# Threshold attention with a feed-forward on one core: the first four head pairs computed with queries on partitions, the first feed-forward blocks ordered one 256-token block at a time, and new ranks

## The chip, the cores and the metric

The kernel runs on one core of one Trainium2 chip. The metric is the time of one execution in microseconds (us). Of the kernel before, three runs are known: 1312.47, 1314.48 and 1315.28 us, median 1314.48 us.

Five engines matter here. TensorE (PE in the profile, its weight loads PEld) multiplies matrices into PSUM, VectorE (DVE) and ScalarE (ACT) work on tiles in SBUF and PSUM, GpSimd (POOL) and SyncE (SP) issue most DMA transfers. The program holds a list of instructions for each engine, which waits on semaphores where it needs another engine's result.

## The reference

There are 8 batches, 8 heads, 576 tokens and head dimension 64; the attention output, 4608 tokens by 512, is the input of a feed-forward of width 2048.

```python
scores = scale * np.matmul(q, k.transpose(0, 1, 3, 2))
thresh = np.max(scores, axis=-1, keepdims=True) - tau
scores = np.where(scores >= thresh, scores, -1000000000.0)
scores = scores - np.max(scores, axis=-1, keepdims=True)
attn = np.exp(scores)
attn = attn / (np.sum(attn, axis=-1, keepdims=True) + 1e-09)
out = np.matmul(attn, v)            # then (B,H,S,D) -> x (B*S, H*D)
h = x @ w_in                        # 512 -> 2048
g = h * (1.0 / (1.0 + np.exp(-1.702 * h)))
return g @ w_out                    # 2048 -> 512
```

q, k and v are float32. The two weight matrices arrive as float64, and the kernel makes float32 of them itself.

## The kernel before

**Pairs.** Two heads form a pair; there are 32 pairs, n = 0 to 31, four to a batch. A pair goes through a row of steps. Its q and k are loaded (`load_qk`, SP) and turned on VectorE (`prep`, L522). The scores are computed with keys on partitions: for each of nine groups of 64 keys, four matmuls of a quarter of the array each (`scores`, L538) fill one of three PSUM buffers called `psA`. ScalarE copies each group to SBUF (`keep`, L555), as five tiles, four of 128x1152 and one of 128x576. The maximum over keys therefore runs across partitions: VectorE reduces while it turns 32x32 blocks (`in_groups`, L561), then over tiles and halves (`over_tiles`, `over_halves`), turns the small result, writes it to DRAM and reads it back spread over all partitions (`row_out`, `row_in`; pair 2 spreads it on VectorE). VectorE subtracts it from the tiles (`sub`, L666), ScalarE masks with a steep Prelu (`mask`, L672) and takes exponentials (`exps`, L676). TensorE multiplies by v (`values`, L687). For pairs 0 to 4 the sums are matmuls with ones (`sums_by_pe`, also L687) that VectorE reduces, inverts and spreads (`one_row`, `spread_sums`); later pairs sum on VectorE and spread through DRAM. `place_x` (L789) writes the normalised result, transposed, into the tiles `xT` of 256 tokens that the feed-forward reads.

**Weights.** 32 pieces of 128x512, 16 of `w_in` and then 16 of `w_out`, are each loaded by two 512 KB transfers from POOL (`load_w`) and converted in four steps: three on VectorE (`cv_ex` L484, `cv_frac` L498 and L502, `cv_end` L510) and one on ScalarE (`cv_power` L492). The first six loads are held back by a small POOL copy (`hold`, L529) that waits until k of pair 3 is turned.

**Feed-forward.** Blocks of 256 tokens. The first two blocks go together as plain matmuls (`first_blocks`): for each of 16 column groups j of `w_in`, four matmuls for block 0 and four for block 1 (`mm1_0`, L844), into a PSUM buffer of the pool `psM`, of which there are two; a tanh on ScalarE and a product on VectorE (`gelu_0`, L850); then the second layer (`mm2`, L826). All of it waits for the four pairs of batch 0. Blocks from 2 on (`feed_forward`, L804 and L995) use seven products in place of eight; block 2 needs pairs 0 to 7.

**Who sets the order.** Nothing is executed as it is written down. Each step is a task with an engine, a planned cost, a rank, prerequisites and buffer counts that it takes and gives (`task`). `run_in_order` plays the tasks through in planned time: an engine that is free takes the ready task of lowest rank whose buffers are free, and the instructions are emitted in that order. Ranks are the pair's number plus a bias by function name from a table: `EARLY` for pairs 0 to 3, `SECOND` for 4 to 7, `LATER`, and `CV` and `W_RANK` for the weights. Feed-forward matmuls have the highest rank and fill what TensorE has left over. From pair 7 on, the values of pair n-2 and the scores of pair n alternate tile by tile.

Of the kernel before, what the change touches and what calls it, by code (L numbers as in the profile page):

```python
# [30 lines left out]
def kernel(  # L31
# [75 lines left out]
        for x in range(2)  # L107
# [9 lines left out]
    minus = const.tile([P, 2, KT], FP32, name="minus")  # L117
    own_row = const.tile([P, QB // 2], FP32, name="own_row")
    shift = const.tile([P, 1], FP32, name="shift")

# [6 lines left out]
    limits = {"psA": 3, "psM": 2, "s_m": 8, "s_t": 2, "io": 2, "hs": 2, "osb": 2, "xT": NXT, "mb": 1,  # L127
              "raw0": 1, "raw1": 1, "qkT0": 1, "qkT1": 1, "v_m0": 1, "v_m1": 1, "w64_0": 1, "w64_1": 1, "row": 1, "row_s": 1, "rc": 1}
    for x in ("raw0", "raw1", "qkT0", "qkT1", "mb"):
        limits[x + "_apart"] = 1  # L130
    limits["s_m_apart"] = NKT

    EARLY = {
        "exps": -17.61,
        "in_groups": 12.77,
        "keep": 26.48,
        "load_qk": 6.42,
        "load_v": 0.46,  # L140
        "mask": 4.73,
        "one_group": -15.86,
        "one_row": -9.06,
        "over_halves": -11.42,
        "over_tiles": -0.06,
        "place_x": -9.61,
        "prep": -11.56,
        "row_in": 31.26,
        "row_out": -12.68,
        "scores_run": 26.41,  # L150
        "spread_max": 4.27,
        "spread_sums": 4.87,
        "sub": 8.56,
        "sums_by_pe": -5.69,
        "sums_in": 2.27,
        "sums_out": 16.51,
        "turn_rows": -16.86,
        "turn_sums": -5.4,
        "values": 24.67,
        "w_sum": 2.1,  # L160
        "x_sum": -20.63,
    }
    SECOND = {
        "exps": -12.92,
        "in_groups": 29.73,
        "keep": 6.19,
        "load_qk": 1.9,
        "load_v": 13.07,
        "mask": 1.29,
        "one_group": 2.55,  # L170
        "one_row": -2.79,
        "over_halves": -24.79,
        "over_tiles": 9.26,
        "place_x": -19.31,
        "prep": -22.42,
        "row_in": -9.56,
        "row_out": -26.33,
        "scores_run": 2.45,
        "spread_max": 6.39,
        "spread_sums": -1.67,  # L180
        "sub": 27.62,
        "sums_by_pe": 38.88,
        "sums_in": 16.9,
        "sums_out": 8.98,
        "turn_rows": 12.04,
        "turn_sums": -0.33,
        "values": 2.02,
        "w_sum": -3.88,
        "x_sum": -12.22,
    }  # L190
    LATER = {
        "exps": 1.49,
        "in_groups": 1.97,
        "keep": -9.78,
        "load_qk": -5.98,
        "load_v": -3.59,
        "mask": 21.95,
        "one_group": 4.78,
        "one_row": -20.84,
        "over_halves": 8.94,  # L200
        "over_tiles": -3.1,
        "place_x": 4.68,
        "prep": -7.1,
        "row_in": 2.23,
        "row_out": -2.52,
        "scores_run": -13.43,
        "spread_max": -3.68,
        "spread_sums": -27.9,
        "sub": 9.4,
        "sums_by_pe": 4.28,  # L210
        "sums_in": 8.55,
        "sums_out": -0.12,
        "turn_rows": -4.72,
        "turn_sums": 8.12,
        "values": 0.63,
        "w_sum": 21.55,
        "x_sum": 7.65,
    }
    CV = {
        "cv_end": -26.29,  # L220
        "cv_ex": 6.34,
        "cv_frac": -13.49,
        "cv_power": -9.91,
        "load_w": 3.03,
# [4 lines left out]
    QUARTERS = ("scores", "scores_run", "again", "values", "sums_by_pe")  # L229
    ENTER = {True: 0.2, False: 0.22}  # L230

    def task(engine, cost, rank, f, *a, after=(), take=(), give=(), lag=None):
        if lag is None:
            lag = LAG[engine]
        if 0 <= rank < LAST:
            biases = EARLY if a[0] < NPAIR else SECOND if a[0] < 2 * NPAIR else LATER
            rank += CV[f.__name__] if f.__name__ in CV else biases.get(f.__name__, 0.0)
        tasks.append((engine, cost, rank, f, a, [x for x in after if x is not None],
                      take, give, lag))
        return len(tasks) - 1  # L240
# [14 lines left out]
    def run_in_order():  # L255
# [30 lines left out]
        while events:  # L286
# [24 lines left out]
            for engine, queue in ready.items():  # L311
# [24 lines left out]
                if engine == "PE":  # L336
                    held_for = follows.get(i)
                    last, mode = mode, tasks[i][3].__name__ in QUARTERS
# [7 lines left out]
    TWICE = ()  # L346
    BY_POOL = {}

    APART = (1, 3)
    spare = arena[:, 8 * P * 4 :]
    offset = {"raw0": 0, "raw1": S, "qkT0": 2 * S, "qkT1": 3 * S, "mb": 4 * S}
    offset.update({f"s_m{t}": (6 + 2 * t) * S for t in range(NKT)})
# [17 lines left out]
    def home(n, tag, key=None):  # L372
        if n in APART:
            o = offset[key or tag]
            return spare[:, o : o + (2 if tag == "s_m" else 1) * S]
        return seat(tag)

    def seat_scores(n, t):

        if t < NKT and n in APART:  # L380
            return home(n, "s_m", f"s_m{t}")
# [13 lines left out]

    def own(n, *pools):
        return tuple(x + "_apart" for x in pools) if n in APART else pools

# [18 lines left out]
    def load_v(n):  # L417
        b, hp = divmod(n, NPAIR)
        t = seat("v_m", n % 2).rearrange("p (h j d) -> p h j d", j=NK, h=2)
# [99 lines left out]
    def prep(n, which):  # L519

        dst = home(n, f"qkT{which}")
        nc.vector.transpose(out=dst, in_=raws.pop((n, which)))  # L522
        mats[n, which] = dst
        if which:
            held_k[n] = dst
# [8 lines left out]
    def scores(n, j):  # L534
# [8 lines left out]
        if j == NK - 1 and n not in TWICE:  # L543
# [33 lines left out]
    def over_halves(n):  # L577
# [7 lines left out]
        if n in TWICE:  # L585
            for x, y in ((0, 0), (1, 2), (2, 1), (3, 3)):
                nc.vector.scalar_tensor_tensor(
                    out=flat[0][ts(y, 32), 0:QB], in0=r[ts(x, 32)], scalar=gap[ts(x, 32)],
                    in1=o[ts(x, 32)], op0=ALU.subtract, op1=ALU.max,
                )  # L590
            return
# [14 lines left out]

    def row_blocks(n):

        nc.vector.transpose(out=flat[1], in_=flat[0])
        mb = home(n, "mb")[:, 0:SH]  # L610
        nc.vector.tensor_tensor(
            out=mb.rearrange("p (g i) -> p g i", i=32),
            in0=flat[1].unsqueeze(1).to_broadcast([P, QB // 2, 32]),
            in1=own_row.unsqueeze(2).to_broadcast([P, QB // 2, 32]), op=ALU.mult,
        )
        mbs[n] = mb

    def again(n, j):
        ps = psA.tile([P, 2, 512], FP32, name="ps", tag="ps")
        for first in (True, False):  # L620
            for h in range(2):
                for c in range(2):
                    if first:
                        left = mats[n, 1][ts(h, D), ts(j, KT)]
                        right = mats[n, 0][ts(h, D), ts(c, SH)]
                    else:
                        left, right = minus[ts(h, D), c, :], mbs[n][ts(h, D), :]
                    nc.tensor.matmul(
# [863 lines left out]
```

## Time and profile before

| what | value |
|---|---|
| median of three runs | 1314.48 us (1312.47 to 1315.28) |
| span of the profiled execution | 1309.8 us |
| median above the span | 4.7 us |
| PE busy over the span | 1260.5 us, 96% |
| DVE, ACT, POOL busy | 1002.2, 646.6, 246.1 us |
| first feed-forward matmul (L844) | at 113.93 us |
| first matmul of block 2 (L804) | at 273.55 us |
| mean granted TensorE clock | 0.989 |

The profile gives the span of the profiled execution, from its first to its last instruction. A run's time also holds what lies around that span; no time of the profiled execution itself is given, so the 4.7 us are the distance from this span to the median of the runs. Busy time is the union of an engine's instructions. The trace holds two records for each f32 matmul, so a count there is twice that of the program. The last batch's end is the end of TensorE's work, so the two marks at 113.93 and 273.55 us cut the span into an attention stretch, a mixed stretch, and the long rest.

### The profile page before, as it was taken

Reading aid. Unit: us, or ns where it says so; the run is one execution under the profiler, and the core shown is the slowest. Engines: PE = TensorE matmul, PEld = TensorE weight load, DVE = VectorE, ACT = ScalarE, POOL = GpSimd, SP = SyncE. Lnnn points to the kernel's source line nnn. Section 1 sums busy time; section 2 is a strip of 40 time slices with the busy share of each in tenths; the row PEclk is TensorE's granted clock in tenths of the full one; section 3 lists DMA queues with packets and bytes.
Section 4 is the critical chain, followed back from the end, with each engine's and each line's share of the span. In section 5 each row is a group of like instructions: output and inputs, shape, how many; then the busy total and the mean of one; then the engine's idle time right before and its main releaser. Section 6 shows DMA issues by size and latency. Waiting matters only on the chain. (4 is left out here: it accounts for less than half of the span.)

```text
span 1309.8 us, 22824 instructions
## 1 busy us (share of the span) xinstructions
PE 1260.5 (96%) x9128; PEld 972.6 (74%) x9128; DVE 1002.2 (77%) x1601; ACT 646.6 (49%) x830; POOL 246.1 (19%) x300
## 2 busy tenths in 40 slices
PE   5869999999999999999999999999999999999998
PEld 2436854477688777777778888777777778888887
DVE  7999998989998877778877877777888864652642
ACT  5975656766664544455554545454556540210210
POOL 1301210022030212112020302020212117120120
PEclk8989999999999999999999999999999999999999
DMA  6976967264322222221222222222122110000000
GB/s 118 339 186 214 282 209 132 67 125 83 82 57 71 55 64 64 56 57 44 63 47 61 55 71 55 72 56 70 42 52 54 38 44 9 9 1 33 1 1 32
DMA packets 194309, 103.78 MB, mean 79 GB/s; under 512 B 160284, under 2 KB 171292, under 8 KB 194204
## 3 DMA queue, kind: packets, MB, share of 16 engines
q1 hardware_dynamic: 180476, 64.30, 20.6%
q0 software_dynamic: 11360, 37.74, 9.7%
q8 instruction: 71, 1.16, 0.4%
q10 hardware_dynamic: 2368, 0.30, 0.2%
q14 instruction: 34, 0.28, 0.1%
HBM read 88.40 MB, written 9.70 MB: 75 GB/s over the span
## 5 line engine op out<-in xcount | busy, mean ns | idle before, releaser
L561 DVE TRANSPOSE_TENSOR_REDUCE part<-arena 128x36 f32<-128x1152 f32 x295 | 361.5, 1241 | 45.9 <-ACT arena L555 32.3
L804 PE MATMUL hps<-xT,w_in 128*128 128x256 f32 x1536 | 336.9, 380 | 0.4 <-DVE arena L816 0.4
L804 PEld LDWEIGHTS hps<-xT,w_in 128*128 128x128 f32 x1536 | 290.8, 190 | 45.5 <-issue 5.7
L672 ACT ACTIVATE arena<-arena 128x1152 f32<-128x1152 f32 (+1 forms) x160 | 169.4, 1058 | 144.9 <-DVE arena L666 144.6
L555 ACT COPY arena<-ps 128x576 f32<-128x576 f32 x288 | 170.4, 647 | 121.2 <-PE ps L538 120.9
L666 DVE TENSOR_TENSOR arena<-arena 128x1152 f32<-128x1152 f32 (+1 forms) x158 | 197.5, 1281 | 19.6 <-DMA arena<-row 19.5
L995 PE MATMUL ops<-w_out,arena 128*128 128x256 f32 x896 | 202.9, 381 | 1.2 <-DVE arena L816 1.1
L676 ACT ACTIVATE arena<-arena,shift,scl 128x1152 f32<-128x1152 f32 (+1 forms) x160 | 200.1, 1251 | 4.1
L538 PE MATMUL ps<-arena 64*64 64x288 f32 x2304 | 174.1, 419 | 25.1 <-DVE arena L522 14.4
L995 PEld LDWEIGHTS ops<-w_out,arena 128*128 128x128 f32 x896 | 169.0, 190 | 29.1 <-DVE arena L816 3.7
L961 POOL TENSOR_TENSOR arena<-arena 128x256 f32<-128x256 f32 x56 | 50.8, 907 | 658.4 <-DVE arena L816 556.7
L687 PE MATMUL pv<-arena 64*64 64x288 f32 x2176 | 161.2, 410 | 0.0
L538 PEld LDWEIGHTS ps<-arena 64*64 64x64 f32 x2304 | 83.7, 137 | 93.6 <-ACT arena L555 30.7
L995 PE MATMUL ops<-arena 128*128 128x256 f32 x672 | 150.6, 380 | 0.0
L813 ACT ACTIVATE th<-hps 128x512 f32<-128x512 f32 x112 | 66.0, 589 | 167.9 <-PE hps L804 148.2
L995 PEld LDWEIGHTS ops<-arena 128*128 128x128 f32 x672 | 127.3, 190 | 19.3 <-issue 2.2
L687 PEld LDWEIGHTS pv<-arena 64*64 64x64 f32 x2176 | 82.0, 135 | 55.3 <-issue 12.8
L1017 DVE SCALAR_TENSOR_TENSOR osb<-ops,osb 128x256 f32<-128x256 f32 x98 | 39.5, 414 | 91.8 <-PE ops L995 85.0
L816 DVE SCALAR_TENSOR_TENSOR arena<-th,hps 128x512 f32<-128x512 f32 x96 | 64.1, 667 | 37.1 <-ACT th L813 37.0
L844 PE MATMUL hps<-xT,w_in 128*128 128x256 f32 x256 | 57.3, 382 | 1.3 <-DVE arena L850 1.2
L826 PE MATMUL ops<-w_out,arena 128*128 128x512 f32 x128 | 56.4, 596 | 0.0
L844 PEld LDWEIGHTS hps<-xT,w_in 128*128 128x128 f32 x256 | 48.1, 190 | 11.0 <-DVE arena L850 3.0
(117 smaller groups left out, 1027.8 us busy)
## 6 DMA issues: line engine op xcount, KB each, us to landing
arena<-in_v_dram SPq DMA_DIRECT2D x128, 144.0 KB
arena<-in_q_dram SPq DMA_DIRECT2D x128, 72.0 KB
out_dram<-osb SPq DMA_DIRECT2D x36, 256.0 KB
arena<-in_k_dram SPq DMA_DIRECT2D x124, 72.0 KB
arena<-row SPq DMA_DIRECT2D x62, 144.0 KB
arena<-row_s SPq DMA_DIRECT2D x54, 144.0 KB
w_out<-in_moe_w_in_dram POOLq DMA_DIRECT2D x12, 512.0 KB, 9.4
arena<-in_moe_w_out_dram POOLq DMA_DIRECT2D x12, 512.0 KB, 5.9
```

The lines of the kernel that those rows point to most:

```text
L538: nc.tensor.matmul(ps[ts(c, KT), h, 0:SH], lhsT=mats[n, 1][ts(h, D), ts(j, KT)], rhs=mats[n, 0][ts(h, D), ts(c, SH)], start=True, stop=True,)
L555: nc.scalar.copy(out=sT[n, t][:, u], in_=pss.pop((n, j))[:, :, 0:SH])
L561: nc.vector.tensor_reduce(out=stats[n, op][:, t * 2 * QB : min(2 * t + 2, NK) * QB], in_=sT[n, t].rearrange("p u h (g d) -> p (u h g) d", ...
L666: engine.tensor_tensor(out=s, in0=s, in1=mbs[n].unsqueeze(1).to_broadcast(list(s.shape)), op=ALU.subtract)
L672: nc.scalar.activation(out=s, in_=s, func=AF.Prelu, alpha=STEEP)
L676: nc.scalar.activation(out=s, in_=s, func=AF.Exp, scale=scl, bias=shift)
L687: nc.tensor.matmul(o[c][ts(h, D), 0:SH], lhsT=left(j, h)[ts(c, KT)], rhs=sT[n, t][ts(c, KT), u, h, :], start=(j == 0), stop=(j == NK - 1),)
L804: nc.tensor.matmul(hidden[j][:, ts(f, BLK)], lhsT=w_in[:, c, ds((f * HF + j) * P, P)], rhs=xTs[blk][:, c, :], start=(c == 0), stop=(c == N ...
L813: nc.scalar.activation(out=ths[j], in_=hidden[j], func=AF.Tanh, scale=GELU_SCALE / 2)
L816: nc.vector.scalar_tensor_tensor(out=g[:, :, j, :], in0=two(ths.pop(j)), scalar=1.0, in1=two(hidden.pop(j)), op0=ALU.add, op1=ALU.mult,)
L844: nc.tensor.matmul(hidden[j][:, ts(i, BLK)], lhsT=w_in[:, c, ts(j, P)], rhs=xTs[i][:, c, :], start=(c == 0), stop=(c == NDC - 1),)
L995: nc.tensor.matmul(banks[blk][k][:, ts(o, HM)], lhsT=left[:, j, :], rhs=right[:, j, :], start=(j == 0), stop=(j == HF - 1),)
```

## The change

1. **Pairs 0 to 3 are computed the other way round.** For each pair and each tile of 128 queries (four whole tiles and one of 64 queries, so 20 units in all) `straight_scores` puts queries on partitions and keys along the row. The row maximum is then one VectorE reduction from PSUM per head (`straight_max`), and its negative plus tau a bias per partition (`straight_bias`). ScalarE masks from PSUM with that bias (`straight_mask`) and takes exponentials with the row sum as a second output (`straight_exps`). Ten transposes by TensorE per whole unit turn the exponentials (`straight_turn`), into one `psA` and one `psM` buffer, ScalarE copies them out (`straight_copy`, `straight_copy1`), VectorE inverts the sums (`straight_rc`), TensorE spreads them (`straight_den`) and multiplies by v (`straight_values`), ScalarE copies the spread (`straight_spread`) and VectorE multiplies (`straight_place`). Gone for these pairs are `keep`, `in_groups`, the trip of the maxima through DRAM, `sub`, the 1152-wide `mask` and `exps`, `sums_by_pe`, `one_row`, `spread_sums` and `place_x`.
2. **Order of units.** Token tiles 0 and 1 of all four pairs come first (units 0 to 7), then tiles 2 to 4. All q and k of the four pairs are loaded first, into the arena; v is loaded twice per pair.
3. **First feed-forward blocks.** The order is now layer 1 of block 0, layer 1 of block 1, layer 2 of each. Block 0 waits only for tiles 0 and 1 of the four pairs.
4. **Ranks and planned costs.** All bias tables, `CV` and `W_RANK` have new numbers, some planned costs are changed, so the emitted order of every engine is new to the end. Pairs 4 to 31 and blocks from 2 on keep their instructions.

```diff
+    def straight_scores(n, t):
+        qT, kT = mats[n, 0], mats[n, 1]
+        ps = [psA.tile([P, 2, 512], FP32, name="ps", tag="ps") for _ in range(heads(t))]
...
+        for h, c, kk in runs:
+            o = t * P + (c * KT if heads(t) == 2 else 0)
+            nc.tensor.matmul(
+                ps[h % heads(t)][ts(c, KT), kk, 0:SH], lhsT=qT[ts(h, D), ds(o, KT)],
+                rhs=kT[ts(h, D), ts(kk, SH)], start=True, stop=True,
+            )
...
+    def straight_max(n, t, h):
+        nc.vector.tensor_reduce(
+            out=figures(n, t, 0)[:, h : h + 1], in_=pss[n, t][h][:, :, 0:SH], axis=AXL.XY, op=ALU.max
+        )
...
+    def straight_mask(n, t, h):
+        nc.scalar.activation(
+            out=probs[n, t][:, h, :].rearrange("p (c s) -> p c s", c=2),
+            in_=pss[n, t][h][:, :, 0:SH], func=AF.Prelu, bias=figures(n, t, 1)[:, h : h + 1],
+            alpha=STEEP,
+        )
+
+    def straight_exps(n, t, h):
+        s = probs[n, t][:, h, :]
+        nc.scalar.activation(
+            out=s, in_=s, func=AF.Exp, scale=scl, bias=shift,
+            accum_out=figures(n, t, 2)[:, h : h + 1],
+        )
+
+    def straight_turn(n, t):
+        big = psA.tile([P, 2, 512], FP32, name="ps", tag="ps")
+        rest = psM.tile([P, BANK], FP32, name="rest", tag="mo")
+        pr = probs.pop((n, t))
+        for h in range(heads(t)):
+            for x in range(4):
+                nc.tensor.transpose(big[:, h, ts(x, P)], pr[:, h, ts(x, P)], eye)
+            nc.tensor.transpose(rest[:, ts(h, P)], pr[:, h, S - P :], eye)
...
+    def straight_values(n, t):
+        to, v_m, k = turned.pop((n, t)), vs[n], P // (3 - heads(t))
+        for x in range(5):
+            for h in range(2):
...
+                nc.tensor.matmul(
+                    small[n, t][ts(h, D), ds(2 * P, k)], lhsT=v_m[:, h, (x + 1) % 5, :], rhs=right,
+                    start=(x == 0), stop=(x == 4),
+                )
...
-    SUMS_BY_PE = (0, 1, 2, 3, 4)
+    SUMS_BY_PE = (4,)
...
-    W_RANK = (0, 15.75, 22.55, 26.06, 2.06, 16.74)
+    W_RANK = (12.68, 4.74, -9.33, 15.31, 8.01, 7.11)
...
+    FIRST_ORDER = ((1, 0), (1, 1), (2, 0), (2, 1))
...
+                xs = [places_0[n, t] for n in range(NPAIR) for t in range(2 * i, 2 * i + 2)]
...
+    HOLD = 3
+    S_RANK = (-1.44, 2.78, 7.37)
...
+            a = task(
+                "PE", 1.0 if whole else 0.6, r, straight_scores, n, t, after=preps[n] + chain[0][-1:],
+                take=("psA",) * heads(t) + (pp,), give=("s_m",) if t == NQT - 1 else (),
+            )
...
+                b = task("DVE", 0.79, r, straight_max, n, t, h, after=[a])
+                b = task("DVE", 0.17, r, straight_bias, n, t, h, after=[b, tau_done])
+                m = task("ACT", 0.64, r, straight_mask, n, t, h, after=[b], give=("psA",))
+                es.append(task("ACT", 0.72, r, straight_exps, n, t, h, after=[m]))
...
+            a = task(
+                "PE", 1.0 if whole else 0.5, r, straight_turn, n, t, after=es + chain[1][-1:],
+                take=("psA", "psM"), give=back,
+            )
...
+    preps = [load_pair(n, 0.5 * n, [], False) for n in range(NPAIR)]
+    tasks[tau_done][5].extend(preps[0])
+    h = task("POOL", 0.3, FIRST, hold, HOLD, after=preps[HOLD][1:])
+    for a in w_loads[0:6]:
+        tasks[a][5].append(h)
+    straight(preps)
+    first_blocks()
```

## The prediction

> **What bounds the kernel now.** I read the slices of the span first, then three stretches, then TensorE's instructions in order of time. Slices (tenths busy, granted clock):
>
> ```profile
> PE   5869999999999999999999999999999999999998
> DVE  7999998989998877778877877777888864652642
> ACT  5975656766664544455554545454556540210210
> PEclk8989999999999999999999999999999999999999
> ```
>
> TensorE has gaps only in the first three slices (to about 100 us); there VectorE is full. The stretches (busy us of PE, PEld, DVE, ACT, POOL, then clock, DMA share, GB/s):
>
> ```profile
> 10.00:112.00 102.00, 73.04 (x988) 39.27 (x984) 98.38 (x167) 82.58 (x104) 18.16 (x33) 0.89 0.77 223
> 112.00:273.50 161.50, 157.46 (x1052) 97.04 (x1045) 146.82 (x238) 94.83 (x121) 21.04 (x34) 0.98 0.64 175
> 273.50:1309.80 1036.30, 1028.76 (x7089) 835.50 (x7087) 754.35 (x1189) 467.68 (x603) 204.15 (x214) 1.00 0.21 50
> ```
>
> To 112 us VectorE is 96.5% busy (98.38 of 102) and TensorE loses 29 us, besides 8.7 before its first matmul. From 112 to 273.5 TensorE loses 4 us, afterwards 7.5 in 1036. So the end is TensorE's list plus what it loses early. Where it loses (start, length, bracket: idle before and who ended it):
>
> ```profile
> 70.13 2.20 PE L687 MATMUL den<-arena,ones 64*64 64x288 f32 x16 [5.01 <-ACT arena L676]
> ...
> 93.41 2.20 PE L687 MATMUL den<-arena,ones 64*64 64x288 f32 x16 [6.79 <-ACT arena L676]
> ...
> 113.93 16.32 PE L844 MATMUL hps<-xT,w_in 128*128 128x256 f32 x74
> ```
>
> It waits for a pair's exponentials, and no feed-forward exists to fill in until the fourth pair is placed, at 113.93.
>
> ```profile
> 273.55 13.98 PE L804 MATMUL hps<-xT,w_in 128*128 128x256 f32 x64
> ```
>
> This first matmul of block 2 is my mark: in both programs scores of pairs 0 to 9, values of 0 to 7 and both first blocks lie before it, and the same instructions after it. I predict by how much the mark moves.
>
> **VectorE, pairs 0 to 3.** Durations are start-to-start times inside runs. Removed per pair: five turning reductions 5.97, five subtractions 5.79, L570 to L605 1.6, L718 to L789 3.2, two preps 1.4: 18.0, in all 72 us. Added: 36 row maxima from PSUM, which no row shows; the nearest are the ScalarE copy of the same 576 columns (0.65) and the turning reduction of 576 on VectorE (0.75). I take the second, being VectorE's, 27 us; with as much again above it the bounds are 23 and 31. 36 biases at 0.17 (6.1), 20 inversions at 0.38 (7.6), 20 products (0.28 at 128 columns, 0.22 at 64: 5.2), preps 6.9 with k in four instructions. Sum 53, so VectorE sheds 19 us.
>
> **ScalarE.** Removed per pair: nine copies at 0.55 (16 took 8.79) and 11.2 for five masks and exponentials: 16.1, in all 64. Added: 36 masks from PSUM, between the copy (0.55) and the 576-wide mask (0.70): 0.66; 36 exponentials at 0.78, the pitch of the 576-wide form, whose row sum no row shows (0 to 0.2 more each, 7 us in all; I take 0); copies of 1024 columns at 1.05, on the line through 256 columns (0.356) and 576 (0.65); the small ones 0.24 to 0.55. Sum 82: ScalarE gains 18 us of work, and so takes VectorE's place beside it as the bound.
>
> **TensorE.** Scores stay (144 matmuls, 17.5 us). Removed: 288 quarter matmuls for sums and values, 34.9 (four side by side per 0.485). Added: values of 128 columns, 64 wide. A record of 256 columns takes 0.219, two make a matmul, so 128 columns take 0.219; two side by side make 0.11 each, none 0.22. Quarters run side by side in every L687 row (16 records of 0.40 each in 0.97), so I take 0.107: 19.3, and 4.4 for the spreads; alone 47. Then 180 transposes: one pass of 128 columns is 0.11, two passes, as each other f32 matmul has, 0.22. I take 0.10 (18 us), since a transpose multiplies nothing; at 0.22 it is 40. TensorE's work grows by 7 us, at most 52. The list also changes the array's shape 75 times up to the last straight product, at about 0.1 each (two L826 at 0.866 and the change behind them took 1.81 at 182.65): 8 us. All of this is costed at nothing on the path: the idle time of this stretch hides it, 45 us by the lists below; what exceeds that comes back one for one.
>
> The Trainium skill, "TensorE: Matmul & The Clock Gate", Part 4 (PE-mode transpose), gives about 275 ns in a kernel's context and says that transposes do not raise the clock; by that the 180 would take 50 us, an estimate, 32 more than the sum has. No run here shows one.
>
> **The lists up to the last straight product.** Counting the changed program's order with these durations: VectorE 123 us (straight work and preps 53, 22 converted weight pieces at 2.02 make 44, seven gelu products 4.6, the rest tau terms and pairs 4 to 6), ScalarE 117 (82, 21 pieces 14, 18 copies 10, seven tanh 4, pair 4 7), TensorE 92 (59, 56 of 128 first-layer matmuls 24.5, scores of pairs 4 to 6 8.7). VectorE begins at 7.2. At the density it has now, 0.965, it is done at 7.2 + 123/0.965 = 134.7. ScalarE begins near 11.6 (scores at 8.9, then a maximum behind the tau terms and a prep) and pays 3 us for v of pair 0 (below); 11.6 + 117 + 3 = 132, and 0.3 per unit for the way over four engines makes 138. I take 137.
>
> **From there to the mark** TensorE's list holds 126 us. The present mixed stretch takes 159.6 for a list of 153 (4% lost, mostly 2.4 at 246 us and 1.6 behind gelu); in the new order pair 7 is placed 234 us into VectorE's list, about 15 before it is needed, so I take 3.5 lost. Mark: 137 + 129.5 = 266.5 against 273.55, **7 us earlier**. At the bounds: ready at 129 gives 258, at 150 gives 280.
>
> **Queues.** SP issues all q and k first: 24 transfers at 0.53 to 0.65 behind the first four, so k of pair 3 leaves by 20 in place of 26.2, and the POOL copy that holds the weights ends near 26 in place of 32.3. The weights then come 6 us sooner, but VectorE wants them sooner too; I count no gain. v of pair 0 moves from 9 us to behind k of pair 3; it lands near 24, and TensorE's list stands before it with the scores of unit 4 behind: the 3 us above. q and k of pair 4 now stand before v of pair 2 while weights load; the like took 8.70 and 6.16 us to issue at 61 to 76 us. v of pair 2 is wanted near 55, so I count 0, at worst 8. Removed row transfers cost nothing: they waited on VectorE.
>
> **After the mark** the instructions are the same under new ranks. Now 7.5 us are lost there; VectorE at 95.8% from 300 to 400 us shows how near a bad order is. I take 0, bounds -4 and +6.
>
> **Sum:** span 1309.8 - 7 = 1302.8; the median stands 4.7 above the profiled span, so 1307.
>
> **Rivals.**
> - *Fewer losses.* VectorE and ScalarE dense, ready near 129, and the mixed stretch without its 4%: the mark 12 to 15 us earlier, 1297 to 1303. For it: ScalarE has 117 of work only; against: VectorE alone needs 130 without one gap.
> - *The gain is swallowed.* The mark moves by less than 2.6, because layer 2 needs all 16 pieces of `w_out` at its first output tile and VectorE converts ten of them after the straight stretch; if these are late by 5, TensorE waits at layer 2 instead: 1312 to 1317.
> - *Transposes of two passes*, 0.22 each: 20 us more on TensorE. Its list is then 112 of the 137, each unit holds `psA` 1.1 longer, and I let 10 surface: ready at 147, 1317. It decides from about 0.18 each. For it: all f32 matmuls here have two records; against: no arithmetic is needed. By the page above it would be worse, near 1325.
> - *Four engines in step* (the slower side by waits alone): a unit goes TensorE, VectorE, ScalarE, TensorE, ScalarE, TensorE, VectorE on three `psA` buffers, of which it takes three. At density 0.88 VectorE ends at 147, mark 276.5, 1317 to 1321. It decides below 0.90 (144). For it: the chain is longer than today's; against: 0.965 now, with weight conversions to fill.
>
> **How the numbers follow.** Three runs lie within 2.8 us, so 0.2% (2.6 us) is about what can be told from no change. Chances: forecast (1303 to 1311) 0.45, fewer losses 0.22, swallowed 0.14, two-pass transposes 0.08, engines in step 0.11. Faster 0.67, same 0.14, slower 0.19. The range 1297 to 1320 takes in all but the tails of the first and the last two.
>
> **What would show it.** Right: the first layer starts between 75 and 90 us in place of 113.93, the last straight product lies at 132 to 142, block 2 starts at 262 to 271, transposes near 0.1, and ScalarE is over 0.9 busy from 12 to 135. Wrong: transposes at 0.2 or more; VectorE below 0.9 busy before 140; TensorE idle at layer 2 behind `cv_end`; more than 10 us lost after block 2 starts.

## The result and the profile after

The changed kernel takes 1327.7 us, median of four runs (1325.9 to 1330.0), against 1314.6 us before (four runs, 1312.5 to 1315.3): ratio 1.0103, 95% interval 1.0086 to 1.0119. It is slower by 13 us; the forecast was 1307, 7 us faster, with a range up to 1320.

Each of these four runs lies 1.7 to 1.8 us above its own span. The profiled execution of the changed kernel (span 1328.3) is the slowest of its four, that of before (1309.8) is a quick one, so the two profiles differ by 18.5 us where the medians differ by 13.1, and some 3 of the 4.7 us between the span of before and its median stand for that quick execution. The slices of the span after (tenths busy, and granted clock, the share of full speed that TensorE was given):

```profile
PE   6798989897999999999999999999999999999998
...
DVE  6888887987788888777787777778887873652642
ACT  6897665676455555555455545455555540210210
...
PEclk9899999898999999999999999999999999999999
```

A slice is 33.2 us. The first three slices read 6, 7 and 9 in place of 5, 8 and 6, but slices 4, 6, 8 and 10 (100 to 332 us) fall to 8 and 7, where before has a 9 from slice 4 on, and the clock is lower in two of them. The same three stretches as before, with the mark (first matmul of block 2, now L886) at 287.45 in place of 273.55 (busy us of PE, PEld, DVE, ACT, POOL, then clock, DMA share, GB/s):

```profile
10.00:112.00 102.00, 90.21 (x955) 61.93 (x948) 85.97 (x208) 90.48 (x176) 21.17 (x39) 0.95 0.74 217
112.00:287.45 175.45, 161.48 (x1167) 99.14 (x1164) 146.21 (x243) 111.84 (x152) 17.91 (x29) 0.96 0.61 161
287.45:1328.30 1040.85, 1029.58 (x7089) 838.05 (x7087) 746.75 (x1181) 458.31 (x593) 209.25 (x214) 1.00 0.21 49
```

To 112 us TensorE is indeed fed better (90.2 busy in place of 73.0). From 112 on it loses 14.0 us where it lost 4.0, at a clock of 0.96 in place of 0.98, and after the mark 11.3 in place of 7.5. TensorE's instructions after its longer waits, in order of time (start, length, bracket: idle before and who ended it):

```profile
50.19 0.66 PE L758 MATMUL rest<-arena,arena 128*64 128x128 f32 x2 [4.15 <-DMA arena<-in_v_dram]
51.41 2.37 PE L758 MATMUL rest<-arena,arena 128*64 128x128 f32 x18 [0.56 <-DMA arena<-in_v_dram]
...
124.98 5.37 PE L929 MATMUL hps<-xT,w_in 128*128 128x256 f32 x17 [3.63 <-DVE arena L935]
...
174.23 1.99 PE L929 MATMUL hps<-xT,w_in 128*128 128x256 f32 x8 [1.94 <-DVE arena L935]
185.09 5.19 PE L929 MATMUL hps<-xT,w_in 128*128 128x256 f32 x15 [1.88 <-DVE arena L935]
...
249.13 2.20 PE L540 MATMUL ps<-arena 64*64 64x288 f32 x16 [5.21 <-ACT arena L557]
...
317.71 12.53 PE L886 MATMUL hps<-xT,w_in 128*128 128x256 f32 x46 [6.04 <-DVE arena L898]
```

L935 and L898 are the gelu products on VectorE. They are short; VectorE came to them late. Its own waits show why:

```profile
121.70 2.63 DVE L627 TENSOR_TENSOR arena<-arena 128x1152 f32<-128x1152 f32 x2 [4.09 <-DMA arena<-row]
...
170.81 1.36 DVE L627 TENSOR_TENSOR arena<-arena 128x1152 f32<-128x1152 f32 x1 [4.95 <-DMA arena<-row]
...
231.24 0.78 DVE L524 STREAM_TRANSPOSE arena<-arena 128x576 f32<-128x576 f32 x1 [5.03 <-DMA arena<-in_k_dram]
...
313.77 0.78 DVE L524 STREAM_TRANSPOSE arena<-arena 128x576 f32<-128x576 f32 x1 [5.87 <-DMA arena<-in_k_dram]
```

Each stands ahead of one of TensorE's waits, by 3 to 4 us and the third by 18: a subtraction waits for the maxima of pair 4 or 5 to come back from DRAM, or a transpose for k of a later pair; a gelu product, or subtractions and then ScalarE's masks and exponentials, stand behind it in the lists; and TensorE waits for those. Pair 6's maxima are waited for too, 3.1 us ahead of 221.65, in front of the third. The waits of VectorE between 112 us and the mark (us in total, times, longest), before and then after:

```profile
DVE arena L666 <- DMA arena<-row: 3.6, 2, 2.7
...
DVE arena L522 <- DMA arena<-in_q_dram: 2.2, 1, 2.2
```

```profile
DVE arena L627 <- DMA arena<-row: 12.3, 4, 4.9
DVE arena L524 <- DMA arena<-in_k_dram: 5.0, 1, 5.0
```

The row trips, and q or k of pair 8, cost VectorE 5.8 us of standing before and 17.3 after.

### The profile page after: what moved, and what is told of

Read it like the earlier page. It is cut to its first block, busy times and chain, and to the rows that moved or that the text cites. A ratio compares the mean times of both kernels' runs of the same rounds, so it can differ in the third digit from the quotient of the medians.

```text
span 1328.3 us, 23115 instructions
## 1 busy us (share of the span) xinstructions
PE 1282.8 (97%) x9212; PEld 999.9 (75%) x9212; DVE 981.8 (74%) x1640; ACT 662.1 (50%) x922; POOL 250.3 (19%) x296
## 4 chain that ended last, share of the span: by engine, by line
PE 78%; DVE 7%; DMA 7%; SPq 4%; ACT 3%; issue 1%; DVEq 0%; ACTq 0%
PE ops L1080 24%; PE hps L886 22%; PE pv L779 8%; PE ps L540 8%; PE ps L994 4%; PE ps L1080 4%; PE ops L994 3%; PE hps L929 3%; SPq L393 2%; DMA arena<-row 2%; DVE arena L627 2%; DVE part L563 2%; DMA arena<-in_k_dram 2%; DMA row<-flat 1%; PE rest L758 1%
## 5 line engine op out<-in xcount | busy, mean ns | idle before, releaser
L563 DVE TRANSPOSE_TENSOR_REDUCE part<-arena 128x36 f32<-128x1152 f32 x275 | 334.5, 1238 | 46.3 <-ACT arena L557 36.9
L886 PE MATMUL hps<-xT,w_in 128*128 128x256 f32 x1536 | 339.7, 382 | 6.9 <-DVE arena L898 6.9
L886 PEld LDWEIGHTS hps<-xT,w_in 128*128 128x128 f32 x1536 | 292.3, 191 | 53.2 <-DVE arena L898 7.9
L633 ACT ACTIVATE arena<-arena 128x1152 f32<-128x1152 f32 (+1 forms) x140 | 147.6, 1059 | 155.6 <-DVE arena L627 155.5
L627 DVE TENSOR_TENSOR arena<-arena 128x1152 f32<-128x1152 f32 (+1 forms) x140 | 178.1, 1313 | 26.7 <-DMA arena<-row 26.6
L557 ACT COPY arena<-ps 128x576 f32<-128x576 f32 x252 | 149.9, 642 | 94.6 <-PE ps L540 92.8
L637 ACT ACTIVATE arena<-arena,shift,scl 128x1152 f32<-128x1152 f32 (+1 forms) x140 | 174.5, 1250 | 3.0
L540 PE MATMUL ps<-arena 64*64 64x288 f32 x2016 | 150.5, 411 | 5.2 <-ACT arena L557 5.2
L779 PE MATMUL pv<-arena 64*64 64x288 f32 x2016 | 147.7, 407 | 0.0
L1080 PEld LDWEIGHTS ops<-arena 128*128 128x128 f32 x672 | 127.2, 190 | 19.3 <-issue 2.2
L540 PEld LDWEIGHTS ps<-arena 64*64 64x64 f32 x2016 | 74.2, 135 | 57.1 <-ACT arena L557 15.9
L898 DVE SCALAR_TENSOR_TENSOR arena<-th,hps 128x512 f32<-128x512 f32 x96 | 64.4, 671 | 38.6 <-ACT th L895 38.4
L929 PE MATMUL hps<-xT,w_in 128*128 128x256 f32 x256 | 62.9, 400 | 7.7 <-DVE arena L935 7.4
L929 PEld LDWEIGHTS hps<-xT,w_in 128*128 128x128 f32 x256 | 49.4, 199 | 19.3 <-DVE arena L935 8.9
L524 DVE STREAM_TRANSPOSE arena<-arena 128x576 f32<-128x576 f32 x60 | 42.9, 746 | 22.1 <-DMA arena<-in_k_dram 11.1
```

Of the source, the lines that this page charges most:

```text
L540: nc.tensor.matmul(ps[ts(c, KT), h, 0:SH], lhsT=mats[n, 1][ts(h, D), ts(j, KT)], rhs=mats[n, 0][ts(h, D), ts(c, SH)], start=True, stop=True,)
L557: nc.scalar.copy(out=sT[n, t][:, u], in_=pss.pop((n, j))[:, :, 0:SH])
L563: nc.vector.tensor_reduce(out=stats[n, op][:, t * 2 * QB : min(2 * t + 2, NK) * QB], in_=sT[n, t].rearrange("p u h (g d) -> p (u h g) d", ...
L627: nc.vector.tensor_tensor(out=s, in0=s, in1=mbs[n].unsqueeze(1).to_broadcast(list(s.shape)), op=ALU.subtract)
L633: nc.scalar.activation(out=s, in_=s, func=AF.Prelu, alpha=STEEP)
L637: nc.scalar.activation(out=s, in_=s, func=AF.Exp, scale=scl, bias=shift)
```

## The experiments

The ratio is to the kernel before on the same chip. The three columns on the right are from the one profiled execution: start of the last straight product, the mark, and the span after the mark. Each run is described under one of the headings below.

| run | us | ratio, 95% interval | last straight | mark | after it |
|---|---|---|---|---|---|
| kernel before | 1314.6 | 1 | | 273.6 | 1036.2 |
| changed kernel | 1327.7 | 1.0103 (1.0086 to 1.0119) | 145.3 | 287.5 | 1040.8 |
| few_turns | 1324.6 | 1.0092 (1.0065 to 1.0118) | 141.1 | 281.9 | 1040.5 |
| no_rowsum | 1326.7 | 1.0108 (1.0086 to 1.0131) | 144.4 | 282.2 | 1040.0 |
| spread45f | 1321.5 | 1.0066 (1.0046 to 1.0087) | 140.2 | 275.7 | 1042.3 |
| v2_first | 1326.8 | 1.0108 (1.0086 to 1.0130) | 141.4 | 280.6 | 1042.3 |
| tail_of_before | 1325.3 | 1.0082 (1.0064 to 1.0101) | 148.1 | 288.3 | 1036.2 |
| spread_tail | 1314.7 | 1.0005 (0.9994 to 1.0016) | 141.0 | 277.1 | 1035.6 |
| late_ffn | 1330.3 | 1.0123 (1.0100 to 1.0146) | 132.6 | 294.6 | 1033.2 |
| st_v2 | 1312.8 | 0.9986 (0.9975 to 0.9997) | 140.2 | 275.1 | 1034.7 |
| st_few_turns | 1310.8 | 0.9969 (0.9958 to 0.9979) | 138.8 | 274.3 | 1035.0 |
| st_no_rowsum | 1312.6 | 0.9981 (0.9970 to 0.9992) | 139.7 | 276.5 | 1036.5 |
| st_pair6 | 1307.2 | 0.9950 (0.9936 to 0.9964) | 142.1 | 270.4 | 1036.9 |
| best_all | 1305.5 | 0.9925 (0.9911 to 0.9940) | 138.8 | 267.1 | 1037.2 |
| before_spread | 1311.9 | 0.9979 (0.9970 to 0.9988) | | 274.4 | 1036.3 |

The columns on the right scatter. Up to the mark tail_of_before has the order of the changed kernel, and its last straight product lies 2.8 us later; no_rowsum has the mark 5.3 us earlier and no better time. So marks that differ by 5 or 7 us between two profiles show no gain by themselves; the ratios have to bear it out.

A changed rank or cost makes the planner write a new order everywhere, which would blur any single edit. So in most runs the planner still plans the changed kernel, and its order is then edited by hand before the instructions are emitted:

```diff
-                tasks[i][3](*tasks[i][4])
+                issued.append(i)
         assert started == len(tasks), (started, len(tasks))
+        for i in edited(issued):
+            tasks[i][3](*tasks[i][4])
```

Line numbers of those kernels are a little higher than those of the changed kernel.

### Less work on TensorE

The run few_turns:

```diff
         for h in range(heads(t)):
-            for x in range(4):
+            for x in range(4 - 4 * h):
                 nc.tensor.transpose(big[:, h, ts(x, P)], pr[:, h, ts(x, P)], eye)
...
-        o, a = to[:, 0:k, :], pss.pop((n, t))[:, 0 : heads(t), :]
+        o, a = to[:, 0:k, :], pss.pop((n, t))[:, 0:1, :].to_broadcast([P, heads(t), 512])
```

> Leaves out part of the computation: of the ten transposes of each of the 16 units with two heads the four wide ones of the second head are not done (64 of 180), and the copy on ScalarE reads the first head's columns twice, so that ScalarE and VectorE have the same work as before. Theory 1 (TensorE's own list bounds the straight stretch: there its instructions took 120 us of the first 145.5, 22 more than forecast with the changes of shape, and from 62 to 112 it was idle for 1.2 us only): 64 x 0.114 = 7.3 us less on TensorE come back nearly whole, last straight product near 139, block 2 starts at 280 to 282 in place of 287.5, time 5 to 8 us under the changed kernel's 1327.7. Rival (ScalarE, or four engines in step, bounds the stretch): TensorE only waits more, at most 2 us.

The ratio is 1.0092 against 1.0103, 1.4 us and within both intervals, where theory 1 had 5 to 8. In the profile the last straight product is 4.2 us earlier and the mark at 281.9, as theory 1 has it, but no_rowsum, below, has the mark at 282.2 with no gain in time. The transposes did fall by 6 us (from 23.5 to 17.3, start to start), but the straight scores rose from 28.3 to 33.1: TensorE ran at half its rate for some 10 us longer at the start. The changed kernel first, then few_turns, same view as above:

```profile
14.77 1.11 PE L708 MATMUL ps<-eye,arena 128*128 128x128 f32 x4
...
19.60 0.66 PE L708 MATMUL ps<-eye,arena 128*128 128x128 f32 x4
```

```profile
20.62 1.12 PE L708 MATMUL ps<-eye,arena 128*128 128x128 f32 x4
...
25.91 4.12 PE L758 MATMUL rest<-arena,arena 128*64 128x128 f32 x40
...
31.09 0.66 PE L708 MATMUL ps<-eye,arena 128*128 128x128 f32 x4
```

Four transposes took 1.11 us until 17 and 0.66 from 19.6 on in the one, 1.12 still at 20.6 in the other. So the run doesn't decide theory 1. It was done again on a base without the row trips of pairs 4 and 5, below; there the half rate ended near 21.5.

### Less work on ScalarE

The run no_rowsum:

```diff
             out=s, in_=s, func=AF.Exp, scale=scl, bias=shift,
-            accum_out=figures(n, t, 2)[:, h : h + 1],
```

> Leaves out part of the computation: the 36 exponentials of the straight units do not sum their rows (the inversion reads another column of the same small table), which takes 36 accumulator readings off ScalarE: 0.09 us of pitch each, 3.3 us in all, 7.2 by their busy time. Theory 1 (TensorE bounds the stretch): the time moves by less than 1.5 us. Rival (ScalarE bounds it, 26.6 of 30 us busy from 10 to 40): block 2 starts 3 to 7 us earlier and the time falls as much.

1.0108: nothing gained, to within some 3 us. The straight stretch ends 0.9 us earlier. The profile has the mark where the rival wanted it, 5.3 us earlier, but not the time. ScalarE alone does not bound the changed kernel.

### No row trip for pairs 4 and 5

The run spread45f:

```diff
     def sub(n, t):
+        if n not in TRIP and t == 0:
+            spread_max(n)
...
+    TRIP = range(6, NP)
```

`row_out`, `row_in` and `turn_rows` do nothing for these pairs; `over_halves` takes its form without a trip.

> The maxima of pairs 4 and 5 are spread by VectorE (a transpose of 0.78 us just before the first subtraction) in place of the row trip through memory; every other instruction keeps its place in each engine's list. Theory 2 (the row trips, 9.4 and 12.0 us from issue to landing, block VectorE's list for 4.1 us at 121.7 and 5.0 at 170.8, and the gelu products behind make TensorE wait 3.6, 1.9 and 1.9): the two waits go, VectorE gains 1.6 of work, block 2 starts 4 to 8 us earlier, at 280 to 283, time 1320 to 1324. Rival (VectorE has slack there and TensorE's list sets the pace): less than 2 us.

The mark came at 275.7, earlier than theory 2 had it, and the time fell by 4.9 us by the ratios. The stretch from the last straight product to the mark:

```profile
140.20:275.70 135.50, 131.50 (x931) 76.08 (x926) 118.17 (x191) 85.24 (x106) 12.69 (x20) 0.97 0.59 145
```

TensorE loses 4.0 us there in place of 9.0: its waits for gelu products fall from 7.4 us to 0.3, that behind the late masks stays (4.0). The straight stretch itself ends 5 us earlier; pair 4's subtraction lay in it. Theory 2 holds. The span after the mark is no shorter.

### v of pair 2 ahead of q and k of pair 4

The run v2_first:

```diff
+        at_v = [i for i in issued if tasks[i][3] is load_v]
+        for w in (0, 1):
+            i = [i for i in issued if tasks[i][3] is load_qk and tasks[i][4][:2] == (NPAIR, w)][0]
+            issued.remove(i)
+            issued.insert(issued.index(at_v[2 + 0]) + 1 + w, i)
```

> On the sync queue v of pair 2 is issued before q and k of pair 4, all else as it is. Theory 3 (q and k of pair 4, 22 us in issue, hold back v of pair 2, TensorE stands 4.7 us at 46 to 51 and its clock falls to 0.74 from 40 to 60): the wait goes and the stretch to 62 us gets 4 to 8 us shorter, block 2 starts at 280 to 283. Rival (the same transfers are only exchanged: q and k of pair 4 land 5 or more later, and their transposes at 48.1 and 49.1 stand in VectorE's list ahead of the straight units' work): between 2 us faster and 4 us slower.

The time stayed (1.0108). The wait for v is gone, and a shorter one has come at the same place. It is behind the transpose of k of pair 4, which ends at 50.41; L742, named as releaser, is the short instruction right behind that transpose:

```profile
49.63 0.78 DVE L534 STREAM_TRANSPOSE arena<-arena 128x576 f32<-128x576 f32 x1 [1.40 <-DMA arena<-in_k_dram]
...
50.56 3.16 PE L550 MATMUL ps<-arena 64*64 64x288 f32 x24 [2.66 <-DVE stat L742]
```

The granted clock is 0.50 from 48 to 56 us here too, so the slow matmuls of this place did not go with the wait for v. The profiled execution has the mark 7 us earlier, but so has no_rowsum, by 5; over the runs nothing is gained, as the rival has it. (Executions of one kernel differ by some 4 us, so times are judged by the ratios.)

### The order of before after the mark

The run tail_of_before:

```diff
+        mark = 938
+        return issued[:mark] + [issued[mark + x] for x in TAIL_ORDER]
```

938 is the place of the first matmul of block 2 in the list. `TAIL_ORDER` puts the tasks behind it into the order that the kernel before has for them.

> The changed kernel up to the first matmul of block 2; from there on every instruction stands in the order that the kernel before has (the 2600 tasks after the mark are the same in both but for some twenty that the changed kernel has done already). Theory 4 (the new ranks of pairs 4 and up give the 4.5 us that are lost after the mark: 1040.8 us there against 1036.3, the largest single wait 6.0 us at 317.7 behind a transpose of k that stood in VectorE's list 5.9 us ahead of its transfer): 1036 to 1037 us after the mark, the mark itself unmoved at 281 to 288, time 3 to 5 us under the changed kernel's. Rival (the loss comes with the state at the mark, weights and row transfers still under way, and not with the order): 1040 or more as now.

```profile
288.30:1324.50 1036.20, 1029.21 (x7089) 835.34 (x7087) 746.74 (x1182) 457.15 (x593) 203.26 (x214) 1.00 0.21 50
```

1036.2 us after the mark, to the tenth what the kernel before has, where the five profiles of the changed order have 1040.0 to 1042.3. Theory 4 is shown: the loss after the mark comes with the new ranks. The time falls by 2.8 us by the ratios, whose intervals overlap.

The same order together with the edit for pairs 4 and 5, spread_tail:

> Both edits at once: the maxima of pairs 4 and 5 spread by VectorE, and the order of the kernel before after the first matmul of block 2. Theories 2 and 4 together: the first edit alone gave a ratio of 1.0066 to the kernel before in place of 1.0103, the mark at 275.7; with 1036 to 1037 us after it the span is 1312 to 1313 and the ratio 1.002 to 1.004. Rival (the two losses are one delay that is only met at another place): the ratio stays at 1.006 or more.

1.0005: the loss is gone, and the program is as fast as before. In the profiles the two edits add up: the first moves the mark (277.1), the second what is behind it (1035.6). By the ratios they give 4.9 and 2.8 us alone and 12.9 together, more than their sum by a little more than the intervals allow; why is not shown.

### The early feed-forward undone

The run late_ffn:

```diff
-                xs = [places_0[n, t] for n in range(NPAIR) for t in range(2 * i, 2 * i + 2)]
+                xs = [places_0[n, t] for n in range(NPAIR) for t in range(NQT)]
```

> The third part of the change undone: the feed-forward of the first two blocks starts only when all four straight pairs are placed, as before; the order is planned anew with the same ranks. If the early feed-forward is what fills TensorE's waits (forecast: first matmul at 75 to 90 in place of 113.9), the first feed-forward matmul starts at 125 to 140, TensorE is under 0.8 busy from 62 to 112 and the mark comes 8 to 20 us later, at 295 to 308. If it only takes TensorE's turns away from the straight units, these end 10 us or more earlier, at 130 to 135, and the mark stays within 5 us of 287.5.

```profile
62.00:112.00 50.00, 42.01 (x524) 28.74 (x523) 42.91 (x107) 46.13 (x94) 9.59 (x19) 1.00 0.66 228
112.00:132.60 20.60, 14.04 (x144) 8.70 (x142) 16.65 (x36) 13.06 (x26) 4.32 (x9) 0.83 0.82 273
132.60:294.60 162.00, 155.16 (x1040) 96.59 (x1035) 138.47 (x226) 98.91 (x122) 14.13 (x22) 0.98 0.58 147
```

Both are true in part. The straight units end at 132.6, 12.7 earlier, with no feed-forward among them on TensorE (0.84 busy from 62 to 112 in place of 0.97). The mark is 7 us later, 162.0 us behind the last straight product in place of 142.2. So the early feed-forward is not where the loss is. What it is worth the run doesn't show: the whole plan is a new one, with 1033.2 us after the mark, and its ratio, 1.0123 from two runs, lies within the interval of the changed kernel's.

### What is left on the base of the two edits

In spread_tail, these stand before TensorE's last long wait ahead of the mark:

```profile
211.63 2.63 DVE L753 TENSOR_TENSOR arena<-arena 128x1152 f32<-128x1152 f32 x2 [2.33 <-DMA arena<-row]
...
220.97 0.78 DVE L643 STREAM_TRANSPOSE arena<-arena 128x576 f32<-128x576 f32 x1 [4.79 <-DMA arena<-in_k_dram]
...
238.17 1.15 ACT L676 COPY arena<-ps 128x576 f32<-128x576 f32 x2
...
238.84 2.20 PE L659 MATMUL ps<-arena 64*64 64x288 f32 x16 [4.96 <-ACT arena L676]
```

VectorE stands for the row of pair 6 and then for k of pair 8, ScalarE's masks and exponentials come late, its copies stand behind them, and TensorE waits for a free `psA`.

First the edit of v2_first on this base, st_v2:

> The two edits that brought the loss down (maxima of pairs 4 and 5 spread by VectorE, the order of before after the mark) and, beside them, v of pair 2 issued ahead of q and k of pair 4. With the row trip of pair 4 out of the way the last straight product lay at 141.0. Theory 3 (the late v costs TensorE 5.8 us at 46 to 52 and half its clock for some 8 us): the last straight product at 136 to 138, the mark at 272 to 274, 3 to 5 us under the 1314.7 of the two edits. Rival (the wait only changes its name, to the transpose of k of pair 4 on VectorE): less than 1.5 us.

Then, in best_all, all that seemed to be waited for; beside the edit of v2_first:

```diff
-    TRIP = range(6, NP)
+    TRIP = range(7, NP)
...
+        i = [i for i in issued if tasks[i][3] is straight_values and tasks[i][4] == (2, 1)][0]
+        issued.remove(i)
+        j = [i for i in issued if tasks[i][3] is straight_values and tasks[i][4] == (2, 0)][0]
+        issued.insert(issued.index(j) + 1, i)
```

> As the run with v of pair 2 first, and two more: pair 6's maxima are spread by VectorE too, which takes its row trip (2.3 us of VectorE's idle time at 209) from in front of q and k of pair 8 on the sync queue (4.8 us of idle at 216 behind k, and 5.0 us of TensorE at 234 to 239 behind the late masks); and TensorE does the product of the second unit of pair 2 ahead of the first scores of pair 4. If the waits are what separates this program from a faster one, the mark comes to 266 to 270 and the time to 1304 to 1309, under both kernels. If the lists are the limit, 1309 to 1313.

And of these the change of `TRIP` alone, st_pair6:

> The two edits, and of the three that the fastest run so far had beside them only the one for pair 6: its maxima too are spread by VectorE, so that no row trip stands in front of q and k of pair 8 on the sync queue. The fastest run had the mark at 267.1 and 1305.5, the two edits alone 277.1 and 1314.7, v of pair 2 first 275.1 and 1312.8. If the row trip of pair 6 and the late k of pair 8 are what made TensorE wait 5.0 us at 234 to 239: no such wait, the mark at 270 to 273, 1308 to 1311. Rival (the gain of the fastest run came from the order at 46 to 52, v first and the product moved ahead): the wait at 234 to 239 stays 3 us or more, the time at 1312 to 1315.

v first gains 2.5 us by the ratios (0.9986 against 1.0005, intervals that just overlap), less than theory 3 said and more than its rival; the last straight product moves by 0.8 only. The row trip of pair 6 gains 7: with it gone, q of pair 8 leaves the sync queue at 199.1 in place of 208.8, and TensorE has no wait from the last straight product to the mark, in st_pair6 and in best_all alike, at a granted clock of 1.00:

```profile
142.10:270.40 128.30, 128.30 (x929) 74.94 (x926) 118.66 (x191) 84.81 (x106) 12.73 (x20) 1.00 0.60 151
```

```profile
138.80:267.10 128.30, 128.30 (x929) 74.93 (x924) 119.26 (x191) 84.76 (x106) 12.62 (x20) 1.00 0.61 151
```

best_all joins both edits, and TensorE does one product of pair 2 (`straight_values`) ahead of the first scores of pair 4. It takes 1305.5 us, 0.75% under the kernel before and 1.8% under the changed one: same arithmetic as the changed kernel but for the way of three pairs' maxima, and another order.

The two edits that take work from TensorE and from ScalarE, as shown above, on the base of spread_tail (st_few_turns and st_no_rowsum):

> Leaves out the four wide transposes of the second head in the 16 units with two heads (the copy reads the first head's twice), on the base of the two edits, so that the row trip of pair 4 does not hide the answer: last straight product at 141.0 in the base. Theory 1 (TensorE's list bounds the straight stretch): 7.3 us less on TensorE, last product at 134 to 135, first feed-forward matmul near 71. Rival (it is one chain over four engines, and TensorE's gain is its next wait): 138 to 141.

> Leaves out the row sums of the 36 straight exponentials (3.3 us of ScalarE by pitch), on the base of the two edits. ScalarE as the bound of the straight stretch: last straight product at 137 to 138 in place of 141.0. TensorE as the bound, or the late v: 140 to 141.

On this base the transposes left out give 0.9969 against 1.0005, 4.7 us, and 3.3 us less on ScalarE 0.9981, 3.2 us (each within 2 us by its interval). The last straight product moves by 2.2 us, as the rival of theory 1 has it, and by 1.3. Neither engine bounds the stretch alone and neither's work is hidden. How much belongs to which isn't settled: 7.3 us of transposes went, but TensorE's instructions up to the last straight product took only 3 us less (118.6 to 115.4), since its half rate at the start lasted until 21.5 in place of 18.4.

### Is it the change's own loss?

The run before_spread is the kernel before, in its own order, with `TRIP = (0, 1, 3, *range(7, NP))` and `spread_max` ahead of the first subtraction of pairs 4, 5 and 6:

> The kernel before with one edit: the maxima of pairs 4, 5 and 6 are spread by VectorE in place of the row trip, every instruction else in its place, as in the fastest runs of the changed kernel. There VectorE stood 0.9 us behind a row of these pairs and 2.3 behind q of pair 8 from 112 to 273.5, against 12.3 and 5.0 in the changed kernel. If the loss of the change lies in where its new order puts the row trips, the kernel before has nothing of the sort to gain: within 2 us of 1314 (the edit adds 1.2 us to VectorE). If row trips cost any order of this kernel as much, it gains 5 us or more and the change is still a loss against it.

```profile
112.01:274.40 162.39, 156.54 (x1064) 95.83 (x1057) 150.01 (x244) 95.10 (x122) 20.99 (x34) 1.00 0.64 171
```

0.9979, 2.8 us gained, and TensorE loses 5.9 us in this stretch, no less than the 4.0 before; where the 2.8 us come from its profile doesn't show. In the changed kernel the same edit for three pairs is worth 17 us (1.0082 to 0.9950, both with the tail of before). So most of the loss belongs to the new order, in which the trips are waited for, and against this kernel too the straight units with the early feed-forward are ahead (0.9950 and 0.9925 against 0.9979), once the order after the mark is that of before.

## Why the prediction was wrong

**Bound and marks (right).** TensorE's list plus what it loses early is the right account, and the mark the right place to read it. The first feed-forward matmul came at 75.7 (forecast 75 to 90), the hold ended at 21.6 (26), row maxima took 0.75 and wide copies 1.02 us, and the 180 transposes ran at 0.108 to 0.114 each, one record per transpose (0.10 was taken, so the rival of two passes fell). The Trainium skill, "TensorE: Matmul & The Clock Gate", Part 4, has about 275 ns for a bf16 transpose in a kernel; this trace has 0.11 us from start to start and 0.28 us as the length of one, which overlap.

**Density of VectorE (wrong in size).** "At the density it has now, 0.965": it was 0.84 from 10 to 112 (85.97 of 102). The list was too long in its turn: VectorE was busy for 115.9 us up to the last straight product in place of 123, and 123 at 0.84 would have ended near 154, so two errors in part made up for each other. The straight stretch ended at 145.3 in place of 137, inside the bounds of 129 to 150 and at the value of the rival with four engines in step (147). Some 5 us of the 8 go with the row trip of pair 4, which lay inside the stretch (140.2 and 141.0 without it; the changed kernel's order had 148.1 in a second profile). I put the other 3 on the chain over the engines, which no run takes apart. TensorE's list there was too short: 92 us (100 with the changes of shape) measured 120, its scores 28.3 in place of 17.5, transposes 23.5 for 18, values 24 for 19.3, where short runs of unlike matmuls, a half-rate start and a half-rate stretch from 46 to 56 us had been priced by long runs at full rate. "All of this is costed at nothing on the path" did not hold: taking work from TensorE gave 4.7 us on the later base.

**The mixed stretch (the step that failed).** "So I take 3.5 lost" on 126 us: it took 142.2, and 137.8 to 140.8 in the four other profiles that keep all the row trips and, behind the straight stretch, the order. Undisturbed, as in best_all, the list is 128.3 with nothing lost, so the list was right within 2.3. The other 13.9 are waits: 9.0 of idle time, and 4.9 of slower matmuls behind them (granted clock 0.83 from 240 to 260, 0.96 over the stretch, 1.00 in best_all). The working asked how far ahead of its need pair 7 was placed on VectorE's list. It did not ask what VectorE itself would wait for: the row trips of pairs 4, 5 and 6 and k of pair 8 had no term in the sum. The planner prices such a trip's second half at 1.1 us to issue, 0.7 us of transfer (2.3 beside a weight transfer, by its `SHARE`) and 1.7 of lag, 5.1 in all. From issue to use it took 10.1 us for pair 4 (111.65 to 121.70) and 12.8 for pair 5 (158.01 to 170.81), while weights, q, k and v moved and the DMA engines were counted as fully busy (share 1.05 and 1.04); for pairs 6 and 7 it took 3.9 (217.73 to 221.65) and 4.0 (233.95 to 237.91), at shares of 0.55 and 0.59. Before, the trip of pair 4 ran under other work: its read was issued at 131.06, its first subtraction came at 145.94, and VectorE stood for 1.4 us in between, for a weight.

**Queues (right place, wrong size).** "I count 0, at worst 8" for q and k of pair 4 ahead of v of pair 2: TensorE stood 4.7 us, and the clock stood at 0.50 for 10 us around it. Undoing it gains nothing alone and 2.5 us on the base of the two edits: what was put behind is then waited for in its turn.

**After the mark (inside the bounds).** 0 was taken, with -4 and +6: it was +4.5, and the runs show that it comes with the new ranks. Of the signs that were to tell the forecast wrong two came: VectorE below 0.9 busy before 140, and more than 10 us lost after block 2 starts (11.3). Of those for it three did not come: the last straight product and block 2 were late, and ScalarE was 0.88 busy from 12 to 135 in place of over 0.9.

**The rivals.** Fewer losses and two-pass transposes fell. The gain was not swallowed by late pieces of `w_out`. Engines in step had the straight stretch and a density below 0.90, and its price of 1317 to 1321 lacked the waits behind it. No rival spoke of transfers that block VectorE's list, though the groups of before listed 19.5 us of VectorE's idle time behind such rows over its span. In one sense the arithmetic stood: in best_all, where these transfers are not waited for, the straight stretch ends at 138.8 (forecast 137), the mark is at 267.1 (266.5) and the time 1305.5 (1307). That this is so close is in part luck: it is another program, with edits found afterwards and the order of before behind the mark, and lists of VectorE and TensorE that were wrong by 7 and 20 us go into it.

## What to carry to other kernels

When a change rewrites the order, ask of each engine's list not only how full it is but what each entry waits for: here a transfer of some microseconds that had run under other work was waited for once the work was moved away, and everything behind it in the list was late with it. Price a round trip through memory by its length beside the transfers that will run then, not by a quiet one. To test one wait, keep the written order and change that one thing; a planner that is given a new cost changes everything.

## What was not expected of the hardware

- TensorE's first matmuls ran at half rate, 0.21 us from start to start per transpose in place of 0.11, while the profile's granted clock reads 1.00: the trace's first entry of that clock is the return to full rate, at 18.68 us in the changed kernel and at 29.52 in few_turns, and a stretch without an entry is read as 1.00. In the runs with all transposes it came at 17.0 to 19.5 us, in few_turns and st_few_turns, which leave 64 of them out, at 29.5 and 21.5. The Trainium skill, "TensorE: Matmul & The Clock Gate", Part 1, puts the half rate at about 3.4 us of sustained work; in few_turns TensorE shows no idle time from 17.9 us on, was busy for 8.00 of the 8 us from 20 to 28, and ran at half rate until 29.5, so there the measurement decides.
- Matmuls beside a wait were slow too. In the stretch with the wait for v of pair 2 (columns as for the three stretches) the changed kernel had

```profile
46.00:56.00 10.00, 5.29 (x42) 3.58 (x44) 7.93 (x19) 7.50 (x15) 0.00 (x0) 0.50 0.55 109
```

  that is half the clock for 10 us around 4.7 us of idle time. The Trainium skill, "TensorE: Matmul & The Clock Gate", Part 1, has the clock fall after an idle window of about 3.4 us. The trace does not show it so here: the record has the fall at 45.99, where the wait of 4.15 us only begins and behind one of 1.66 us, and in v2_first, where TensorE worked on from 44.6 to 47.9 us, it has the fall at 45.93 all the same.
- The row sum as a second output of the exponential is an instruction of its own in the trace, 0.2 us long and 0.09 us of pitch, 36 times.
